# Loads, masks and the start of MLP1 rearranged in the opening of a strided sparse attention + MLP kernel

## The chip, the cores and the metric

One core of one Trainium2 chip. The metric is the device time of one execution in microseconds; the lower, the better. The engines are called PE (TensorE; PEld is its weight load), DVE (VectorE), ACT (ScalarE), POOL (GpSimd) and SP (SyncE, which only issues transfers here). [...]

## The reference

Attention over q, k and v of shape (8, 8, 576, 64): of the eight heads the first four are "local" (a row sees itself and the 31 rows before it), the last four "strided" (a row sees the rows before it at multiples of 32). Then a dense two-layer MLP over the 4608 rows.

```python
scores = scale * np.matmul(q, k.transpose(0, 1, 3, 2))
mask_local   = (rel >= 0) & (rel < 32)
mask_strided = (rel >= 0) & (pos[None, :] % 32 == pos[:, None] % 32)
scores = np.where(masks, scores, -1e9); attn = softmax(scores)
x = (attn @ v) as (4608, 512)
h = x @ w_in                      # 512 -> 2048
g = h * np.tanh(log1p(exp(h)))    # Mish
out = g @ w_out                   # 2048 -> 512
```

## The kernel before, in words

**Work.** Batch b's attention gives 576 rows of x, written transposed into a ring `xT` of four batches. The MLP goes over nine blocks t of 512 rows. `mlp1(t)` (line 435) makes h transposed in eight groups of two 512-column accumulators, eight matmuls each (two 128-row pieces of the output, four 128-deep pieces `cc` of the contraction; `cc` 2 and 3 are the strided heads, 0 and 1 the local ones), and ACT's Mish takes each group to `gT`. MLP2 of block 0 (`mlp2`, line 549) is 16 steps of four matmuls with `w_out` by its four pieces in turn (`fc_major`); blocks 1 to 8 use a seven-product scheme (`mlp2_seven`). The attention of batch t+1 is cut into steps (`attn_steps`, line 376) that are woven between the steps of block t's MLP2.

**Attention of one batch** (`class Attn`). The scores are made for short windows: strided units are 72 by 72, local ones 128 keys by 96 queries. `qk` (line 276) makes the scores of one of three parts in PSUM and ACT takes their exp into `P_s` or `P_l`; `mask` (line 298) multiplies by a 0/1 mask (DVE, or POOL in later batches); `pv` and `pv2` (lines 323, 335) make the output with the denominator as a 65th column, and DVE divides into `x_s` or `x_l`; `xt` (line 349) transposes into `xT`. q and k must first be transposed into `qTs`, `kTs`, `qTl`, `kTl`: on PE by `t_step` (line 212) and, for batch 0's local heads, `t_step_loc0` (line 244), for batches 0 and 1; by the DMA engines from batch 2 on (`transpose_by_dma`, line 185, six transfers on SP).

**Order.** Everything is issued in an order written out by hand (`manual_schedule`); each engine runs its list in that order. The opening is lines 635 to 726: SP loads batch 0's strided q and k as fp32 into `st0` (four transfers of 72 rows and two heads), its v (`vs32`, then `vl32` in two transfers), then batch 1's local q and k as fp32; POOL clears `P_l` and loads batch 0's local q and k with a cast on the way (`lq0`). DVE clears `kTs`, `P_s` and columns of ones. Then follow casts, transposes, scores, masks and outputs of batch 0, strided heads first. POOL's queue carries after that `w_in` in five pieces (held back by one-element copies into `held` until batch 0's v is cast), batch 1's strided q and k, and the first two of the four pieces of `w_out`; the rest of `w_out` and batch 2's strided q and k wait for `cast_v1` (line 728), which runs in step 0 of block 0's MLP2. On SP a small transfer `gate` (line 709) that reads the end of `w_in` holds back what stands behind it: batch 1's v, then batch 2's local q and k, then batch 2's v, and the six DMA transposes of batch 2 (put into step 9).

**PSUM.** `acc(i)` gives three accumulators of two banks, `tile_t` two tiles of one bank that transposes (`tr`, `trx`) and single outputs (`po`) share.

**MLP1 of block 0** comes after the whole attention of batch 0. Its first two groups take `cc` 2, 3 before `cc` 0, 1. Batch 1's transposes follow groups inside MLP1: local ones after the sixth and seventh, the first strided ones after the last (line 758).

Of the kernel before, what the change touches and what calls it, by code (L numbers as in the profile page):

```python
# [15 lines left out]
STRIDE = 32  # L16
# [5 lines left out]
RING = 4  # L22


def _consts():

    kk = np.arange(128)[:, None]
    qq = np.arange(WQ)[None, :]
    rel = qq + 32 - kk
    p = np.arange(PN)  # L30
    c = np.zeros((128, 128 + WQ + PN), np.float32)
    c[:, 0:128] = np.eye(128)
    c[:, 128:128 + WQ] = (rel >= 0) & (rel < STRIDE)
    c[:PN, 128 + WQ:] = (p[:, None] % 4 == p[None, :] % 4) & (p[:, None] <= p[None, :])
    return c.astype(ml_dtypes.bfloat16)
# [3 lines left out]
def kernel(ctx, tc, q, k, v, moe_w_in, moe_w_out, out):  # L39
# [15 lines left out]
    consts = const.tile([128, 128 + WQ + PN], BF16, name="consts_sb")  # L55
    ident = consts[:, 0:128]
    loc = consts[:, 128:128 + WQ]
    stm = consts[0:PN, 128 + WQ:128 + WQ + PN]
    vl32 = const.tile([128, 4, NW, D], F32, name="vl32")
# [55 lines left out]

    def load_qk_loc(b):
        for dst, src in ((kl32, k), (ql32, q)):
            if b < 2:
                nc.sync.dma_start(
                    dst[0:PL].rearrange("p h j d -> p h (j d)"),  # L120
                    src[b, 0:4].rearrange("h (p j) d -> p h (j d)", j=CL),
                )
            else:
                nc.sync.dma_start(
                    dst[0:PL].rearrange("p h i d -> p (h i) d"),
                    src[b, 0:4].rearrange("h (i p) d -> p (h i) d", p=PL),
                )
# [40 lines left out]
    def cast_qk_loc(b, e_k, e_q):  # L168
        for e, dst, src in ((e_k, kl, kl32), (e_q, ql, ql32)):
            if b < 2:  # L170
                cast(e, dst[b % 2][0:PL].rearrange("p j h d -> p h j d"), src[0:PL])
            else:
                to = by_tile(dst[b % 2])
                for hp in range(2):
                    cast(
                        e, to[:, hp].rearrange("p i e d -> p e i d"), src[0:PL, 2 * hp:2 * hp + 2]
                    )
# [34 lines left out]
    def t_step(b, kind, which, hp, eng=None):  # L212
# [17 lines left out]
        else:  # L230
            src = (ql if which == "q" else kl)[b % 2]
            for j in range(CL):
                nc.tensor.transpose(
                    tr[:, PL * j:PL * j + PL],
                    src[0:PL, j, 2 * hp:2 * hp + 2, :],
                    ident[0:PL, 0:PL],
                )
# [6 lines left out]
    def t_step_loc0(src, dst, hp, eng):  # L244

        tr = tile_t("tr")[:].bitcast(BF16)
        for j in range(CL):
            for e in range(2):
                nc.tensor.transpose(
                    tr[64 * e:64 * e + 64, PL * j:PL * j + PL], src[0:PL, 2 * hp + e, j, :],  # L250
                    ident[0:PL, 0:PL],
                )
        cast(
            eng, dst.rearrange("c (p j) -> c p j", j=CL),
            tr[:, 0:S].rearrange("c (j p) -> c p j", j=CL),
        )

    T_ORDER = [(kd, w, hp) for kd in ("s", "l") for hp in range(2) for w in ("k", "q")]

    def t_steps(b):  # L260
        return [lambda a=a: t_step(b, *a) for a in T_ORDER]
# [10 lines left out]
    class Attn:  # L272
# [3 lines left out]
        def qk(self, parts, i_acc):  # L276

            ps, o = acc(i_acc, "ps"), 0
            todo = []
            for kind, i in parts:  # L280
                w = WQ if kind == "l" else PN
                o0 = o
                for x, y in PARTS[kind][i]:
                    for e in range(2):
# [6 lines left out]
                        nc.tensor.matmul(ps[:, e, o:o + w], lhsT=lhsT, rhs=rhs, start=True, stop=True)  # L291
# [84 lines left out]
    def attn_steps(b, x, y):  # L376
# [7 lines left out]
        if x == y:  # L384
            return [
                [], [Q(x, s0)],
                [M(*s0), Q(x, s1)],
                [V("s", 0)],
                [V("s", 1), M(*s1), Q(x, *sl2)],
                [V("s", 2)],  # L390
                [V("s", 3), M("s", 2), M("l", 2), Q(x, l0)],
                [V("s", 4)],
                [V("s", 5), M(*l0), Q(x, l1)],
                [V("s", 6), V("l", 5)],
                [V("s", 7), V("l", 0), M(*l1)],
                [X("s", 0), V("l", 1)],
                [X("s", 1), V("l", 2)],
                [V("l", 3), V("l", 4)],
                [X("l", 0), X("l", 1)], [],
            ], {}  # L400
# [34 lines left out]
    def mlp1(t, accs):  # L435
# [5 lines left out]
        def group(g, ccs=(2, 3, 0, 1)):  # L441
# [20 lines left out]
            if ccs[-1] == 1:  # L462
# [3 lines left out]
                if 0 < t < B - 1 and g == 7:  # L466
# [3 lines left out]
        if t == 0:  # L470
            return gT, Sg, [lambda g=g, c=c: group(g, c) for c in ((2, 3), (0, 1)) for g in range(2)] + [
                lambda g=g: group(g) for g in range(2, 8)
            ]
# [159 lines left out]
    with tc.manual_schedule():  # L633
# [6 lines left out]
        for st, src in zip(st0, (k, q)):  # L640
            for h in (0, 2):
                nc.sync.dma_start(
                    st[:, h:h + 2, :],
                    src[0, 4 + h:6 + h].rearrange("h (p j) d -> p h (j d)", j=CS),
                )
        load_v_str(0)
        load_v_loc(0)
        load_qk_loc(1)
        lq0 = g_pool.tile([128, 16, 512], BF16, tag="Sg", name="lq0")
        lq0 = lq0[:].rearrange("p a b -> p (a b)")[0:PL]  # L650
        kl0, ql0 = [lq0[:, 1536 * i:1536 * i + 1536].rearrange("p (h x) -> p h x", h=4) for i in range(2)]
        for p in P_l:
            Po.memset(p[:], 0.0)
        for dst, src in ((kl0, k), (ql0, q)):
# [161 lines left out]
```

## Time and profile before

| | us |
|---|---|
| runs shown | 318.87, 313.11, 316.52; median 316.52 |
| the profiled execution | 314.8 |
| its span | 313.0 |
| PE busy | 291.7 |
| first PE transposes begin | 5.42 |
| PE waits for batch 0's local k until | 13.23 |
| MLP1 of block 0 begins | 25.90 |
| MLP2 of block 0 begins | 42.3 |
| MLP1 of block 1 begins | 63.5 |
| PE waits for the last DMA transpose of batch 2 until | 85.62 |

The span runs from the first to the last instruction that the profile shows; the time of the execution holds 1.8 us more. In a timeline row the first number is the start, the second the length (of a run of merged instructions: from the first start to the last end), then engine, line, operation, result<-operands and count; brackets hold the idle time of the engine before it and what ended that. A row of the waits has who waited for whom, the total, the number of times and the longest. The times of matmuls are pipelined, so that their lengths overlap; the distance of their starts tells their rate.

### The profile page before, as it was taken

What the parts mean: (1) busy time and instruction counts of PE and PEld (TensorE: products, weight loads), DVE (VectorE), ACT (ScalarE), POOL (GpSimd) and SP (SyncE); (2) the same over time, 40 slices, a digit from 0 to 9 for tenths busy, and PEclk for the clock granted to TensorE, in tenths of its full rate; (3) what the DMA queues carried; (4) which work ended last, traced back from release to release, by engine and by line L of the source; (5) the groups of instructions that cost most, each with busy time, mean ns of one, the idle gap of its engine ahead of it and who ended that gap; (6) DMA issues with size and microseconds to landing.
All of it is one profiled execution on the core that took longest, in us unless ns stands there. A gap on an engine that the chain in (4) does not pass through costs nothing.

```text
span 313.0 us, 6764 instructions
## 1 busy us (share of the span) xinstructions
PE 291.7 (93%) x2856; PEld 199.1 (64%) x2856; DVE 158.8 (51%) x362; ACT 172.8 (55%) x220; POOL 103.4 (33%) x112
## 2 busy tenths in 40 slices
PE   1678998999599999999999999999999999999995
PEld 1554454545487468746888887468745884685485
DVE  5572166866435176517642765276527652720542
ACT  3583563476454676557645765576557655514530
POOL 5486018092039402930293029202920230000000
PEclk9999999999979999999999999999999999999999
DMA  6999999999999999999999999899550011003003
GB/s 171 217 245 206 226 201 182 173 176 154 183 232 189 126 253 182 193 124 251 186 152 116 253 177 163 177 191 203 90 172 2 3 67 69 0 2 134 0 2 134
DMA packets 103261, 46.77 MB, mean 149 GB/s; under 512 B 85184, under 2 KB 96000, under 8 KB 103232
## 3 DMA queue, kind: packets, MB, share of 16 engines
q1 hardware_dynamic: 91792, 37.22, 66.1%
q0 software_dynamic: 11152, 8.92, 19.1%
q8 instruction: 22, 0.36, 0.5%
q10 hardware_dynamic: 288, 0.21, 0.2%
q14 instruction: 7, 0.06, 0.1%
HBM read 38.34 MB, written 9.44 MB: 153 GB/s over the span
## 4 chain that ended last, share of the span: by engine, by line
PE 81%; DMA 8%; DVE 4%; SPq 3%; ACT 1%; issue 1%; POOL 1%; POOLq 0%
PE psh L455 29%; PE pso L529 26%; PE psb L455 8%; PE po L318 4%; PE pso L584 4%; DMA lq<-in_k_dram 3%; PE ps L291 3%; DMA w_out<-in_moe_w_out_dram 2%; PE pso L557 2%; DMA qTl<-ql 2%; SPq L187 2%; PE trx L357 2%; SPq L193 1%; PE trx L367 1%; DVE x_l L344 1%; DVE osb L508 1%
## 5 line engine op out<-in xcount | busy, mean ns | idle before, releaser
L455 PE MATMUL psh<-xT,w_in 128*128 128x512 bf16 (+1 forms) x496 | 103.1, 361 | 0.2
L455 PEld LDWEIGHTS <-w_in 128*128 128x128 bf16 x640 | 61.8, 98 | 59.1 <-issue 2.1
L465 ACT ACTIVATE gT<-psh 128x1024 bf16<-128x1024 f32 x56 | 57.1, 1023 | 49.7 <-PE psh L455 49.7
L302 POOL TENSOR_TENSOR Pl<-Pl,consts_sb 128x960 bf16<-128x960 bf16 (+1 forms) x18 | 29.2, 1635 | 104.6 <-ACT Pl L296 104.6
L481 DVE TENSOR_TENSOR Sg<-gT 128x256 bf16<-128x256 bf16 (+2 forms) x64 | 27.0, 422 | 57.4 <-ACT gT L465 55.1
L529 PEld LDWEIGHTS <-Sg 128*128 128x128 bf16 x448 | 42.5, 99 | 6.8
L529 PE MATMUL pso<-Tw,Sg 128*128 128x256 bf16 x336 | 41.6, 279 | 0.0
L529 PEld LDWEIGHTS <-gT 128*128 128x128 bf16 x336 | 31.3, 98 | 4.7
L164 ACT COPY xT<-trx 128x576 bf16<-128x576 bf16 x32 | 20.1, 638 | 23.6 <-PE trx L367 16.7
L164 ACT COPY osb<-pso 128x512 f32<-128x512 f32 (+1 forms) x26 | 14.2, 544 | 31.7 <-PE pso L529 16.0
L455 PE MATMUL psb<-xT,w_in 128*128 128x512 bf16 (+1 forms) x144 | 30.3, 355 | 0.0
L529 PE MATMUL pso<-w_out,gT 128*128 128x256 bf16 x224 | 27.8, 272 | 0.0
L296 ACT ACTIVATE Pl<-ps 128x960 bf16<-128x960 f32 (+1 forms) x24 | 19.4, 806 | 13.9 <-PE ps L291 13.6
L508 DVE TENSOR_TENSOR osb<-pso,osb 128x512 f32<-128x512 f32 x21 | 14.5, 692 | 21.4 <-PE pso L529 21.4
L296 ACT ACTIVATE Ps<-ps 72x864 bf16<-72x864 f32 (+1 forms) x24 | 18.5, 803 | 6.0 <-PE ps L291 5.9
L461 ACT ACTIVATE gT<-psb 128x512 bf16<-128x512 f32 x32 | 19.0, 596 | 3.5 <-PE psb L455 3.5
L344 DVE TENSOR_TENSOR x_s<-po,rden 72x512 bf16<-72x512 f32 x28 | 19.2, 687 | 1.0
L302 DVE TENSOR_TENSOR Ps<-Ps,consts_sb 72x864 bf16<-72x864 bf16 (+1 forms) x24 | 13.8, 574 | 11.3 <-ACT Ps L296 10.7
L557 PE MATMUL pso<-w_out,gT 128*128 128x512 bf16 x64 | 16.4, 379 | 0.5 <-DMA w_out<-in_moe_w_out_dram 0.5
L318 PEld LDWEIGHTS <-Ps 72*128 72x128 bf16 x256 | 12.9, 103 | 5.9 <-DVE Ps L302 2.5
L318 PE MATMUL po<-vs,Ps 72*128 72x65 bf16 x256 | 14.8, 201 | 1.4 <-DVE x_s L344 0.5
L329 DVE RECIPROCAL rden<-po 96x4 f32<-96x4 f32 (+1 forms) x24 | 4.2, 177 | 22.0 <-PE po L318 21.8
(89 smaller groups left out, 341.5 us busy)
## 6 DMA issues: line engine op xcount, KB each, us to landing
out_dram<-osb SPq DMA_DIRECT2D x16, 512.0 KB, 5.1
vl<-in_v_dram SPq DMA_DIRECT2D x7, 768.0 KB
vs<-in_v_dram SPq DMA_DIRECT2D x8, 576.0 KB
kl<-in_k_dram SPq DMA_DIRECT2D x7, 576.0 KB, 9.9
ql<-in_q_dram SPq DMA_DIRECT2D x7, 576.0 KB, 13.7
w_out<-in_moe_w_out_dram POOLq DMA_DIRECT2D x4, 512.0 KB, 14.2
ks<-in_k_dram POOLq DMA_DIRECT2D x7, 288.0 KB, 5.9
qs<-in_q_dram POOLq DMA_DIRECT2D x7, 288.0 KB, 7.8
```

Source lines behind the costliest of these rows:

```text
L164: nc.scalar.copy(out_, in_)
L296: nc.scalar.activation(pt[0:n, :, 0:nw], ps[0:n, :, o0:o0 + nw], AF.Exp, scale=scale)
L302: meng.tensor_tensor(out=pm, in0=pm, in1=mk[0:n, :].unsqueeze(1).unsqueeze(1).to_broadcast([n, 2, nu, w]), op=ALU.mult,)
L318: nc.tensor.matmul(po[:, h, :], lhsT=pt[0:n, c0:c0 + 128], rhs=rhs, start=True, stop=True,)
L344: nc.vector.tensor_tensor(out=dst.rearrange("p e (h d) -> p e h d", h=4), in0=po[0:m, :, :, 0:D], in1=rden[0:m].unsqueeze(3).to_broadcast( ...
L455: nc.tensor.matmul(ps_u[:, o:o + n], lhsT=w_in[:, cc, fc * 128:(fc + 1) * 128], rhs=xT[:, cc, a:a + n], start=(cc == 2 and (o == 0 or len( ...
L461: nc.scalar.activation(gT[:, g + 8 * u, :], ps_u[:], AF.Mish)
L465: nc.scalar.activation(to, tiles[g][:], AF.Mish)
L481: nc.vector.tensor_tensor(out=out_, in0=in0, in1=in1, op=op)
L508: add = lambda o, p: nc.vector.tensor_tensor(out=o, in0=p, in1=o, op=ALU.add)
L529: nc.tensor.matmul(ps[:, pair, :], lhsT=lhs(c, 128 * pair), rhs=rhs(c), start=(first and pair == 0 and c == 0), stop=(last and c == 7), sk ...
L557: nc.tensor.matmul(p[:, ot % 2, :], lhsT=gT[:, fc, 128 * ot:128 * ot + 128], rhs=w_out[:, fc, :], start=(fc == 0), stop=(fc == 15),)
```

## The change

All of it concerns the opening, MLP1 and MLP2 of block 0 and the loads of batches 0 to 2.

- Batch 0's strided q and k are loaded, still as fp32, in pieces of 64 rows (two heads) and 8 rows (four heads); v's strided part likewise in 64 and 8 rows; `vl32` in two halves.
- Local q and k of batches 0 and 1 are loaded by POOL with the cast on the way, straight into `kl` and `ql` (`load_early_loc`); `t_step_loc0`, the fp32 loads and the casts for batch 1 are gone. `t_step`'s local branch now makes 12 transposes of 64 columns instead of 6 of 128.
- Batch 0's masks are no longer multiplied in: a matmul with the identity first puts 0 or -30000 into the PSUM tile, and the scores accumulate on it (`bias`).
- Clearing is cut to the columns that are read without being written; POOL clears no `P_l`.
- `unread(n)` adds n matmuls on a tile of zeros, whose result is not read: nine before the first transposes, two later.
- POOL's queue has one order: five pieces of w_in (released by the first half of `vl32`), first piece of w_out, batch 1's strided q, k, second piece of w_out, batch 1's local q, k, last two pieces of w_out, batch 2's strided q, k.
- SP's gate reads an earlier piece of w_in; a second gate, on w_out's third piece, holds batch 2's local q and k; batch 2's v comes after its transposes (`load_rest2`).
- MLP1 of block 0: `cc` 2, 3 of three groups (12 matmuls) are put between the local outputs of batch 0; two of batch 1's strided transposes close MLP1, the other two open MLP2, and its four local ones go into steps 5 to 8 of MLP2.

```diff
+    def by_head(x):
+        return x[0:PL].rearrange("p j h d -> p (j h d)").rearrange("p (h x) -> p h x", h=4)
+    def load_early_loc(b):
+        for dst, src in ((kl, k), (ql, q)):
+            nc.gpsimd.dma_start(by_head(dst[b]), src[b, 0:4].rearrange("h (p j) d -> p h (j d)", j=CL))
...
+    def unread(n):
+        tr = tile_t("un")
+        for _ in range(n):
+            nc.tensor.matmul(tr[:], lhsT=zeros[:, 0:128], rhs=zeros[:], start=True, stop=True)
...
+        def bias(self, kind, i, i_acc):
+            nu = len(PARTS[kind][i])
+            n, w, mb = (128, WQ, loc_bias) if kind == "l" else (PN, PN, stm_bias)
+            ps = acc(i_acc, "ps")
+            for e in range(2):
+                nc.tensor.matmul(
+                    ps[:, e, 0:nu * w].rearrange("p (u c) -> p u c", u=nu),
+                    lhsT=ident[0:n, :], rhs=mb.unsqueeze(1).to_broadcast([n, nu, w]),
+                    start=True, stop=False, skip_group_check=True,
+                )
+            return ps
...
         if x == y:
+            T = [(lambda n=n, eng=eng: t_step(b, *T_ORDER[n], eng)) for n, eng in enumerate(
+                (None, None, None, None, None, nc.scalar, None, nc.scalar))]
             return [
-                [], [Q(x, s0)],
+                T[2:4], [Q(x, s0)],
...
-                [V("s", 1), M(*s1), Q(x, *sl2)],
-                [V("s", 2)],
-                [V("s", 3), M("s", 2), M("l", 2), Q(x, l0)],
-                [V("s", 4)],
-                [V("s", 5), M(*l0), Q(x, l1)],
-                [V("s", 6), V("l", 5)],
-                [V("s", 7), V("l", 0), M(*l1)],
-                [X("s", 0), V("l", 1)],
-                [X("s", 1), V("l", 2)],
-                [V("l", 3), V("l", 4)],
-                [X("l", 0), X("l", 1)], [],
-            ], {}
+                [V("s", 1), M(*s1), Q(x, ("s", 2))],
+                [V("s", 2), T[4]],
+                [V("s", 3), M("s", 2), T[5]],
+                [V("s", 4), T[6]],
+                [V("s", 5), T[7]],
+                [V("s", 6), Q(x, l0)],
+                [V("s", 7), M(*l0), Q(x, l1)],
+                [X("s", 0), V("l", 0), M(*l1), Q(x, ("l", 2))],
+                [X("s", 1), V("l", 1), M("l", 2)],
+                [V("l", 2), V("l", 3)],
+                [V("l", 4), V("l", 5)],
+                [X("l", 0), X("l", 1)],
+            ], T[0:2]
...
         for st, src in zip(st0, (k, q)):
-            for h in (0, 2):
-                nc.sync.dma_start(st[:, h:h + 2, :], src[0, 4 + h:6 + h].rearrange("h (p j) d -> p h (j d)", j=CS))
+            src = src[0, 4:8].rearrange("h (p j) d -> p h (j d)", j=CS)
+            for p0, p1, h0, h1 in ((0, 64, 0, 2), (64, PN, 0, 4), (0, 64, 2, 4)):
+                nc.sync.dma_start(st[p0:p1, h0:h1, :], src[p0:p1, h0:h1, :])
...
+        unread(9)
+        ps = []
         for hp in range(2):
             h = 2 * hp
             cast(Dv, ks[0][0:PN, h:h + 2, :], st0[0][:, h:h + 2, :])
             t_step(0, "s", "k", hp, Sc)
+            ps.append(a.bias("s", hp, hp))
...
-        Po.tensor_copy(held[:], vs[0][0:1, 3, 0, 0:4])
+        Po.tensor_copy(held[:], vl32[0:1, 1, 5, 0:4])
         load_w_in(0, 256)
         load_w_in(256, 512)
         load_w_in(512, 1024)
-        cast_v_loc(0, Po, 0, 3)
         load_w_in(1024, 1536)
+        for h in (0, 2):
+            cast(Po, vl[0][:, :, h:h + 2, 0:D], vl32[:, h:h + 2].rearrange("p h w d -> p w h d"))
+        Po.memset(vl[0][0:32, 0, :, 0:D], 0.0)
         load_w_in(1536, 2048)
...
+        load_w_out(0, 1)
         load_qk_str(1)
-        load_w_out(0, 2)
-        nc.sync.dma_start(gate[:], w_in[0:1, 0, 1536:1792])
+        load_w_out(1, 2)
+        load_early_loc(1)
+        load_w_out(2, 4)
+        nc.sync.dma_start(gate[:], w_in[0:1, 0, 1024:1280])
         load_v(1)
...
-        a.pv2("l", 0, 1)
-        a.mask("l", 2, Dv)
-        a.pv2("l", 2, 0)
-        a.pv("l", 4)
-        a.pv("l", 5)
-        a.xt("l", 0)
+        a.pv2("l", 0, 0)
+        g1s[0]()
+        a.pv("l", 2)
+        a.pv("l", 3)
+        g1s[1]()
+        a.pv("l", 4)
+        a.xt("l", 0)
+        a.pv("l", 5)
+        g1s[2]()
         a.xt("l", 1)
...
+        load_qk_str(2)
+        nc.sync.dma_start(gate[:], w_out[0:1, 8, 0:256])
         load_qk_loc(2)
...
+        def load_rest2():
+            transpose_by_dma(2)
+            load_v(2)
+            load_qk_str(3)
+            cast_v(2, Po, Po)
```

## The prediction

> **What bounds the kernel now.** I read the page first (span, busy shares, the slices), then the table of busy time by stage, then the waits, then the timeline of the places that the waits name.
>
> ```profile
> span 313.0 us, 6764 instructions
> ...
> PE 291.7 (93%) x2856; PEld 199.1 (64%) x2856; DVE 158.8 (51%) x362; ACT 172.8 (55%) x220; POOL 103.4 (33%) x112
> ...
> PE   1678998999599999999999999999999999999995
> ```
>
> TensorE is busy 93% of the span; what it does not fill, 21.3 us, lies in the first slices, in one slice at about 80 us and at the very end. The stages (columns: length; busy us of PE, PEld, DVE, ACT, POOL; clock; DMA share; GB/s):
>
> ```profile
> 0.00:26.00 26.00, 13.75 (x221) 11.13 (x222) 15.91 (x40) 13.67 (x19) 16.71 (x26) 1.00 1.03 211
> 26.00:42.00 16.00, 16.00 (x97) 7.65 (x95) 2.85 (x4) 7.83 (x10) 2.18 (x3) 1.00 1.24 218
> 42.00:63.50 21.50, 20.31 (x236) 11.39 (x233) 15.40 (x41) 10.47 (x13) 7.79 (x11) 1.00 1.19 181
> 63.50:79.00 15.50, 15.50 (x81) 7.70 (x79) 10.37 (x17) 10.90 (x14) 9.50 (x10) 1.00 1.24 162
> 79.00:102.00 23.00, 19.48 (x247) 15.44 (x246) 10.82 (x24) 10.84 (x15) 9.92 (x9) 0.93 1.25 202
> ```
>
> The opening (attention of batch 0, until MLP1 starts) leaves PE idle 12.25 us, of which 5.4 pass before the first transposes. MLP1 (26 to 42) is full. MLP2 with batch 1's attention woven in (42 to 63.5) lacks 1.2 us. From 79 to 102 PE lacks 3.5 us. After that nothing is to be had that this change touches. The waits of PE after 42:
>
> ```profile
> PE ps L291 <- DMA qTl<-ql: 3.3, 1, 3.3
> PE pso L557 <- DMA w_out<-in_moe_w_out_dram: 0.5, 1, 0.5
> ```
>
> So the hole at 82 to 85.6 is batch 2's last DMA transpose landing late; the other is a piece of w_out. How MLP1 begins:
>
> ```profile
> 15.32 0.98 PEld L249 LDWEIGHTS <-lq 96*64 96x64 bf16 x24
> 24.90 0.99 PEld L357 LDWEIGHTS <-x_l 96*128 96x128 bf16 x12 [1.14 <-DVE x_l L330]
> 25.90 11.58 PE L455 MATMUL psh<-xT,w_in 128*128 128x512 bf16 x48
> 26.32 0.15 PEld L455 LDWEIGHTS <-w_in 128*128 128x128 bf16 x1 [0.28 <-issue]
> 26.75 0.15 PEld L455 LDWEIGHTS <-w_in 128*128 128x128 bf16 x1 [0.28 <-issue]
> 28.03 8.96 PEld L455 LDWEIGHTS <-w_in 128*128 128x128 bf16 x42 [0.28 <-issue]
> ```
>
> The weight loads stand 0.43 us apart until 28.03 and 0.213 apart after it (8.96 over 42): the first five matmuls of MLP1 run at half speed, 5 x 0.21 = 1.07 us lost. The 96-column transposes say the same: 41 ns each at 15.32, 83 ns at 24.90.
>
> **Step 1, the opening up to the end of MLP1.** Before: MLP1 ends at 41.96, by the chain of waits.
>
> Off POOL goes the clearing of P_l (2.25 us), so the two local loads are issued at about 0.75 instead of 2.94; they landed 10.3 and 11.0 us after issue, and PE waited 1.6 us for the first (until 13.23). That wait can go. What is late next is DVE: kTl's two copies (0.76 each) now stand behind the cast of vs, which began at 12.89 and took 1.23. So kTl is ready at 14.12 + 1.52 = 15.6 where ACT had it at 15.15, and q's copies end near 16.8 instead of 17.24. The masks leave DVE (0.60 x 2 + 0.45 + 0.65 x 2 + 0.35 = 3.3 us), of which the chain holds only 0.27. In their place PE gets 12 bias matmuls, 4608 columns together, at 0.216 us for 512 (MLP1's 1.73 us for 8) 1.94 us: half of them in PE's gaps of 0.6 to 0.7 us between the casts, half in front of the local scores, where ACT's copies are waited for. The nine unread matmuls (9 x 0.43 = 3.9 us) fill the empty 1.3 to 5.2, ahead of the first transposes at 5.42; without that cover they would cost what sticks out. SP issues 11 transfers, 0.42 us each, ahead of its gate instead of 9 (batch 1's two fp32 loads go, of which one held SP for 10.38); their data queue anyway. POOL casts vl behind four issues of w_in (0.75 each): 14.7 + 3.0 + 2 x 0.83 + 0.3 = 19.7, and the first local output needed it at 21.54, so 1.8 us cover it. Splitting 72 rows in 64 and 8 has no row in this trace; the four st loads released their casts 1.3 us apart, so it can be worth between +0.5 (the small pieces) and -1. I take the last product of x_s at its old time, 20.96, with -1.5 to +1.0 as bounds.
>
> From there: twelve of MLP1's 64 matmuls now run among the local outputs, 12 x 0.216 = -2.6. The half-speed start goes, -1.07. Two pairs of local transposes leave MLP1 (0.51 x 2), -1.02. The local rows are pushed: DVE has 0.89 + 4 x 0.59 instead of 2 x 0.89 + 2 x 0.59, +0.3, and of the 2.6 us of matmuls put between them PE's old gaps there (0.63 + 0.98) hide 1.6, +1.0. And the twelve may run at half speed as PE did at 24.90: between 0 and +2.6; part lies under DVE's products, I take +0.6. Sum -2.8: MLP1 ends at 39.2 (36.5 to 42).
>
> [...]
>
> **Step 2, batch 1's strided q and k.** Their first transposes now close MLP1, and in POOL's queue they stand behind w_in and a first piece of w_out. Before, w_in, ks, qs and two pieces of w_out (2048 + 576 + 1024 KB) took from the issue at 14.73 to the landing 20.6 us after 22.69, 43.3: 128 KB per us. Now 2048 + 512 + 576 KB come first: 24.5 us. The issue hangs on half of vl instead of on the cast of vs; whole vl released its cast at 17.86, the cast of vs ended at 14.12, so I leave 14.7 (13 to 18). qs is there at 39.2, when MLP1 ends (35 at the 204 GB/s that the windows from 26 to 36 show, 43 with the later issue and v of batch 1 beside it: SP's first gate opens one piece of w_in earlier, near 29 instead of 32.27). Two pieces of transposes, 0.52: MLP2 starts at 39.7 instead of 42.48, -2.8.
>
> [...]
>
> **Step 3, MLP2 of block 0.** It took 42.48 to 63.64. Four local transpose steps of 12 come in: 24 took 1.17, so +2.3. The wait for w_out (0.5) goes, as all of w_out is issued ahead: -0.5. The steps share two PSUM tiles with the outputs, and their copies (0.64 ACT, 0.76 DVE) add waits, between 0 and 4 x 0.4: I take +0.4. Sum +2.2 (+1.5 to +4).
>
> **Step 4, the hole at 82.** Batch 2's local q and k wait at a second gate (w_out's third piece, near 50) but land by the row of ql (9.9 to 13.7 us) at 61 to 65, as before (ql's cast began at 63.20). Batch 2's v now goes behind the six transposes, so their first issue no longer sits 10.03 us in a full queue, and the last, behind ql's cast of 2.7 us, can land near 72 instead of 85.6: -3.3. Then v is late next: issued near 71, landing 9 to 11 us later by the loads at 33.0 and 88.23, cast on POOL in 1.9 to 2.6, needed at 81. The new wait is 0 to 3.3; I take 0.5. Sum -2.8.
>
> **Sum:** -2.8 + 2.2 - 2.8 = -3.4. The profiled execution took 314.8 (span 313.0 and 1.8 around it): 311.4. The median of the runs shown, 316.52, stands 1.7 above that execution, the lowest, 313.11, 1.7 below.
>
> **Rivals.** (a) The hole only changes its name: v of batch 2 takes the 3.3 us. For it: SP issues v after transposes that wait for POOL; against: the queue is emptier then. -2.8 + 2.2 = -0.6: 314.2. (b) The opening is limited by its loads, and these come earlier: x_s 1.5 sooner, no half speed (0.6), no waits in MLP2 (0.4) and none at the hole (0.5): -6.4, 308.4. For it: the wait of 1.6 for the local loads; against: DVE's queue behind the cast of vs. (c) Slower: POOL's one queue falls behind PE. Behind qs come 2112 KB until w_out's last piece, which PE reaches at step 12 of 16, about 18 us later: it takes 117 KB per us. Before, w_out's second half, ks and qs (1600 KB, from 45.90 to 61.6) came at 102, w_out's piece alone (512 KB in 7.4 us) at 69, the last 1088 KB of them at 131. At 85 PE waits 6.8: 318.2. It decides below 99 KB per us, where the wait exceeds 3.4.
>
> **How the numbers follow.** Forecast 0.47 (309 to 313.5), (a) 0.20 (313.5 to 315.5), (b) 0.22 (305.5 to 309), (c) 0.11 (315.5 to 321). Leaving out the ends of (b) and (c), 306 to 317.5 holds eight in ten. Two per cent, about what a measurement of this kernel can tell from no change, is 308.5 and 321.1 against 314.8. Faster: 0.20 of (b) and 0.09 of the forecast's low end, 0.29; slower 0.04; the rest 0.67.
>
> **What would show it.** MLP1's last matmul near 39 and no half-speed spacing after it begins in earnest; no wait of PE on ks or qs over 1 us; MLP2 of block 0 some 2 us longer; no wait on a transpose of batch 2, and POOL's cast of vs done by 81. Wrong would be a long wait of PE on w_in, ks, qs, kl, ql or w_out between 22 and 62 (c), or on vs near 80 (a).

## The result, and the profile after

The changed kernel takes 336.88 us (median of 4 runs, 335.59 to 337.47), the kernel before on the same chip 317.47 (4 runs): a ratio of 1.0695, 95% interval 1.0584 to 1.0807. It is slower by 7%, where 311.4 was forecast and 317.5 was the upper end of the range. Some executions of a kernel are slower than the rest of them, so the ratios are of the others alone (of the kernel before 313.11 and 316.52) and differ from those of the medians, and of the profiled executions only e1's (322.88) is such a slow one. The profiled execution of the changed kernel took 336.94, its span 335.2, 22.2 more than the span before.

Both kernels pass the same marks on PE, so the 22.2 can be put into stages (starts of the first matmul of each MLP part in the timelines):

| stage | before | after | difference |
|---|---|---|---|
| up to the start of MLP2 of block 0 | 42.32 | 47.78 | +5.46 |
| MLP2 of block 0 | 21.16 | 41.58 | +20.42 |
| MLP1 of block 1 | 13.81 | 14.78 | +0.97 |
| MLP2 of block 1 | 22.53 | 17.42 | -5.11 |
| the rest | 213.2 | 213.6 | +0.4 |

The page shows the big loss at once, as a hole in PE's row (a slice is 8.4 us). The row PEclk is at half in two places, from 8 to 33 us and around the hole:

```profile
span 335.2 us, 6848 instructions
...
PE   5498899404899999999999999999999999999995
...
PEclk9555999955999999999999999999999999999999
```

The first of these is no loss against the kernel before. There the same row records the full clock, yet 24 transposes of local k take 1.17 us in both (at 13.23 before, at 18.31 here). Later, at full speed, twelve of this form take 0.31 of weight loads (at 55.40), and here 24 take 0.98 in both. From 11 to 28 us both kernels run at the slow rate.

PE's waits, and the timeline of PE around the longest (here and below rows of a timeline are chosen, and others may stand between two of them):

```profile
PE ps L301 <- DMA qTl<-ql: 17.6, 1, 17.6
PE tr L227 <- DVE ks L176: 5.1, 2, 4.2
PE tr L227 <- DVE qs L176: 1.8, 1, 1.8
```

```profile
62.47 0.29 PE L331 MATMUL po<-vs,Ps 72*128 72x65 bf16 x4
80.40 0.58 PE L301 MATMUL ps<-qTl,kTl 64*128 64x96 bf16 x10 [17.64 <-DMA qTl<-ql]
80.92 1.89 PE L572 MATMUL pso<-w_out,gT 128*128 128x512 bf16 x4
82.60 0.69 PE L380 MATMUL trx<-consts_sb,x_s 72*128 72x72 bf16 x8
83.09 0.42 PE L331 MATMUL po<-vl,Pl 128*128 128x65 bf16 x4
```

The instruction that waits is a local score part (L301) of batch 1, and what it waits for is a DMA transpose into qTl. The rows after it show who it belongs to: batch 1's outputs with vl follow directly. Batch 1's q and k were transposed by PE; the only DMA transposes of this stretch are batch 2's. In the listing, `load_rest2` stands in step 9 of `at`, and batch 1's second and third local score parts stand in steps 10 and 11. There is one kTl and one qTl, so in program order batch 2's transposes come first, and these two parts wait for them. They are then made from batch 2's q and k, so the changed kernel does not give batch 1's local heads the scores that the reference asks for. In the kernel before all local score parts stand in steps up to 8, ahead of the transposes.

Why the transposes are late can be read from POOL's and SP's timelines:

```profile
43.05 0.73 POOL L120 DMA_DIRECT2D qs<-in_q_dram  x1 [3.73 <-DMA ks<-in_k_dram]
61.06 1.59 POOL L176 CAST vl<-vl 128x768 bf16<-128x768 f32 x2 [17.29 <-DMA vl<-in_v_dram]
66.75 1.60 POOL L176 CAST kl<-kl 96x768 bf16<-96x768 f32 x2 [3.84 <-DMA kl<-in_k_dram]
69.11 1.60 POOL L176 CAST ql<-ql 96x768 bf16<-96x768 f32 x2 [0.77 <-DMA ql<-in_q_dram]
```

```profile
33.10 0.38 SPq L154 DMA_DIRECT2D vl<-in_v_dram  x1
55.97 0.54 SPq L752 DMA_DIRECT2D gate<-w_out  x1
56.56 0.57 SPq L130 DMA_DIRECT2D kl<-in_k_dram  x1
57.19 5.73 SPq L130 DMA_DIRECT2D ql<-in_q_dram  x1
63.08 5.00 SPq L194 DMA_TRANSPOSE kTs<-ks  x1
74.83 1.25 SPq L200 DMA_TRANSPOSE qTl<-ql  x1
```

SP's second gate waits for w_out's third piece, which POOL issued at 31.99, and held batch 2's local loads until 55.97. Batch 1's vl, issued at 33.10, landed at 61; POOL's casts of batch 2 stand behind it, but it did not decide: after it POOL still waited 3.84 us for kl and 0.77 for ql to land. The last transpose went out at 74.83 and landed 5.4 us later. From 33 to 61 POOL's queue (q0) and SP's (q1) shared the 16 engines like this (packets, MB, share):

```profile
q0 software_dynamic: 4403, 3.75, 82.2%
q1 hardware_dynamic: 4463, 1.64, 38.5%
```

SP's queue, with 256-byte rows of v, moved 59 KB per us (1.64 MB in 28 us); in the kernel before, from 33 to 48, it moved 124 (1.86 MB in 15) beside a share of 51.2% for POOL's queue. From 40 to 54 the packet counts agree, 2328 of SP's to 2333 of POOL's, and SP's queue, with the smaller packets, moved the smaller part (0.71 MB to 2.01). Before and after that the counts were not equal (366 to 1116 from 33 to 40, 1769 to 954 from 54 to 61), and the near equality of the whole is chance.

The opening's loss begins at the first casts. DVE's casts of the strided q and k, which were at 4.67, 5.95, 7.31 and 8.70:

```profile
5.35 0.69 DVE L176 CAST ks<-st 72x1024 bf16<-72x1024 f32 x1 [3.05 <-DMA st<-in_k_dram]
10.37 0.69 DVE L176 CAST ks<-st 72x1024 bf16<-72x1024 f32 x1 [4.32 <-DMA st<-in_k_dram]
13.59 0.69 DVE L176 CAST qs<-st 72x1024 bf16<-72x1024 f32 x1 [2.54 <-DMA st<-in_q_dram]
14.46 0.69 DVE L176 CAST qs<-st 72x1024 bf16<-72x1024 f32 x1 [0.18 <-DMA st<-in_q_dram]
```

Between 4 and 6 us SP's queue, on which they depend, all but stood still while the local loads of POOL ran (first fence: after; second: before, in the same 2 us):

```profile
q0 software_dynamic: 359, 0.27, 112.3%
q1 hardware_dynamic: 9, 0.02, 2.7%
```

```profile
q1 hardware_dynamic: 248, 0.43, 80.2%
q0 software_dynamic: 5, 0.00, 9.6%
```

Here the counts were far from equal, SP's 9 packets to POOL's 359. What sets the shares of the two queues is not shown.

### The profile page after: what moved, and what is told of

Same layout as the page of the kernel before. It is cut to its first block, busy times and chain, and to the rows that moved or that the text cites. A ratio compares the mean times of both kernels' runs of the same rounds, so it can differ in the third digit from the quotient of the medians.

```text
span 335.2 us, 6848 instructions
## 1 busy us (share of the span) xinstructions
PE 299.2 (89%) x2882; PEld 200.9 (60%) x2903; DVE 153.8 (46%) x363; ACT 172.3 (51%) x219; POOL 97.6 (29%) x108
## 4 chain that ended last, share of the span: by engine, by line
PE 71%; DMA 15%; issue 6%; DVE 3%; SPq 1%; POOL 1%; ACT 1%; POOLq 0%
PE pso L544 25%; PE psh L471 24%; PE psb L471 8%; DMA w_out<-in_moe_w_out_dram 7%; PE pso L599 4%; DMA ql<-in_q_dram 4%; PE po L331 3%; DMA w_in<-in_moe_w_in_dram 3%; PE ps L301 3%; DMA qTl<-ql 2%; PE trx L380 1%; SPq L200 1%; PE pso L572 1%; PE trx L370 1%; DVE x_l L357 1%
## 5 line engine op out<-in xcount | busy, mean ns | idle before, releaser
L544 PE MATMUL pso<-Tw,Sg 128*128 128x256 bf16 x336 | 40.1, 273 | 0.0
L301 PE MATMUL ps<-qTl,kTl 64*128 64x96 bf16 x192 | 9.1, 218 | 17.7 <-DMA qTl<-ql 17.6
L176 POOL CAST vl<-vl 128x768 bf16<-128x768 f32 x16 | 12.9, 836 | 17.9 <-DMA vl<-in_v_dram 17.9
L301 PEld LDWEIGHTS <-kTl 64*128 64x128 bf16 x192 | 5.4, 100 | 19.9 <-DMA kTl<-kl 17.7
```

Of the source, the lines that this page charges most:

```text
L544: nc.tensor.matmul(ps[:, pair, :], lhsT=lhs(c, 128 * pair), rhs=rhs(c), start=(first and pair == 0 and c == 0), stop=(last and c == 7), sk ...
```

## The experiments

All times below are medians beside the kernel before on the same chip (315.5 to 316.1), and the marks are of each kernel's profiled execution:

| | MLP2 of block 0 begins | it takes | MLP1 of block 1 takes | MLP2 of block 1 takes | MLP1 of block 2 begins |
|---|---|---|---|---|---|
| before | 42.32 | 21.16 | 13.81 | 22.53 | 99.82 |
| before again (b0) | 43.27 | 20.64 | 13.81 | 23.14 | 100.86 |
| after | 47.78 | 41.58 | 14.78 | 17.42 | 121.56 |
| e1 | 46.88 | 22.83 | 14.78 | 18.04 | 102.53 |
| e2 | 45.67 | 22.09 | 14.78 | 18.08 | 100.62 |
| b1 | 45.13 | 24.76 | 13.81 | 17.41 | 101.11 |
| b2 | 45.89 | 24.32 | 13.81 | 17.42 | 101.44 |
| e3 | 43.80 | 22.32 | 14.79 | 17.72 | 98.63 |
| e4 | 43.50 | 24.28 | 13.81 | 17.42 | 99.01 |
| e5 | 43.17 | 22.24 | 14.78 | 18.23 | 98.42 |
| e6 | 45.30 | 22.09 | 14.78 | 18.14 | 100.31 |
| e7 | 42.66 | 22.18 | 13.81 | 19.48 | 98.13 |
| e8 | 42.04 | 23.16 | 14.78 | 18.62 | 98.60 |
| e9 | 42.02 | 23.50 | 14.49 | 18.13 | 98.14 |

The program is nearly the same in before, b0, e4 and e7 until MLP1 ends; their 42.32 to 43.50 is what one execution differs from another in this mark. A difference of less than 1.2 us in it between two of the rows shows nothing by itself.

**e1: batch 2's transposes two steps later.**

```diff
-                at[9].append(load_rest2)
+                at[11].append(load_rest2)
```

> The changed kernel with batch 2's transposes and loads (load_rest2) moved from step 9 of block 0's MLP2 to step 11, behind the last local scores of batch 1. Order theory: PE's wait of 17.6 us came from the place of the transposes in the order alone; it goes, MLP2 of block 0 takes about 24 us instead of 41.6, and the time falls from 336.9 to about 319.5, since the opening stays 5.3 late. Rival (late loads): the loads behind are late anyway, PE waits for other pieces instead, and the time stays above 328.

Measured 319.56, ratio 1.014 (1.0083 to 1.0198). PE's wait for a DMA transpose is now 1.0 us in all and falls on a later batch, at 122.66. Batch 1's three parts come before batch 2's transposes, as in the kernel before:

```profile
60.38 0.39 PE L301 MATMUL ps<-qTl,kTl 64*128 64x96 bf16 x10
61.89 0.39 PE L301 MATMUL ps<-qTl,kTl 64*128 64x96 bf16 x10
64.31 0.26 PE L301 MATMUL ps<-qTl,kTl 64*128 64x96 bf16 x4
```

One line of order is worth 17.3 us, of 19 to 21 that the change lost. The rival, that late loads would keep it over 328, falls: loads just as late (vl at 61.4, batch 2's casts of kl and ql at 66.0 and 68.8) cost only one wait of 0.58 us, on vl, where no reader of the tiles stands behind them.

**e2: e1, and POOL clears P_l before the local loads, as before.**

```diff
+        for p in P_l:
+            Po.memset(p[:], 0.0)
         load_early_loc(0)
```

> As e1, and POOL clears P_l (2.25 us) ahead of the first two local loads, as before the change; the 64 and 8 rows stay. Contention theory: the casts of batch 0's strided q and k, at 5.35, 10.37, 13.59 and 14.46 in the changed kernel, come back to near 4.7, 6.0, 7.3 and 8.7, MLP1 ends 5 us sooner, time about 314. Rival (pieces): the small pieces of 8 rows make the loads late; the last cast stays after 13, time about 319.

Measured 317.91, ratio 1.01 (1.0055 to 1.0146); the last strided cast at 11.80 instead of 13.96 (14.46 in the changed kernel). Between the two expectations: the local loads' head start is a part of the loss, not all.

**b1: the kernel before with its local loads ahead of the clearing; b2: the kernel before with the strided q, k in 64 and 8 rows.**

```diff
+        for dst, src in ((kl0, k), (ql0, q)):
+            Po.dma_start(dst, src[0, 0:4].rearrange("h (p j) d -> p h (j d)", j=CL))
         for p in P_l:
             Po.memset(p[:], 0.0)
-        for dst, src in ((kl0, k), (ql0, q)):
-            Po.dma_start(dst, src[0, 0:4].rearrange("h (p j) d -> p h (j d)", j=CL))
```

```diff
-            for h in (0, 2):
-                nc.sync.dma_start(st[:, h:h + 2, :], ...)
+            for p0, p1, h0, h1 in ((0, 64, 0, 2), (64, PN, 0, 4), (0, 64, 2, 4)):
+                nc.sync.dma_start(st[p0:p1, h0:h1, :], src[p0:p1, h0:h1, :])
```

> The kernel before, with only the order of POOL's opening turned round: the two local loads first, the clearing of P_l after them. Contention theory: the four strided casts slip by 3 to 6 us and the time rises from 316 to about 320. Rival (pieces): the strided casts stay within 0.5 us and the wait for local k (1.6 us) goes: 314.5 to 316.

> The kernel before, with only batch 0's strided q and k loaded in 64 and 8 rows. Contention theory: the casts stay within 0.7 us, time the same within 1 us. Pieces theory: the last cast slips from 8.7 to 12 or later, time 319 or more.

Measured 315.93 (ratio 1.0051, 1.0006 to 1.0097) and 318.0 (1.0078, 1.0029 to 1.0127). The last cast moves from 8.70 to 10.53 by the first, to 11.78 by the second (b1's fence first). So each contributes; b1's 1.8 is less than its theory's 3 to 6, and its time stays in the rival's range:

```profile
10.53 0.69 DVE L166 CAST qs<-st 72x1024 bf16<-72x1024 f32 x1 [2.38 <-DMA st<-in_q_dram]
```

```profile
11.78 0.69 DVE L166 CAST qs<-st 72x1024 bf16<-72x1024 f32 x1 [2.68 <-DMA st<-in_q_dram]
```

SP's timeline suggests why the second costs: six issues take 3.8 us where four took 1.7 (b2 first, then before), so that the last of them goes out behind the start of POOL's, at 2.94. No run tries this apart from the pieces themselves.

```profile
0.75 1.99 SPq L643 DMA_DIRECT2D st<-in_k_dram  x3
2.78 1.77 SPq L643 DMA_DIRECT2D st<-in_q_dram  x3
```

```profile
0.75 0.83 SPq L642 DMA_DIRECT2D st<-in_k_dram  x2
1.62 0.83 SPq L642 DMA_DIRECT2D st<-in_q_dram  x2
```

The two add: 8.70 + 1.83 + 3.08 = 13.6, and e1 and the changed kernel, which have both, have 13.96 and 14.46. Yet neither kernel is 3 us slower in the end. MLP2 of block 0 begins 2.8 and 3.6 later in them than in the first profile and takes 3.2 to 3.6 more (with waits of 2.7 and 2.3 on w_out), but then MLP2 of block 1 takes 5.1 less: the transposes of batch 2 come at their own time, and a late PE doesn't meet them. By the start of MLP1 of block 2 only 1.3 and 1.6 us are left: a late opening of the kernel before costs little, because it ends in the hole at 82.

**e3: e1 with all that the change did to the first loads undone** (72 rows, v whole, P_l cleared on POOL first, w_in held by the cast of vs; two places of the edit are shown).

```diff
-            for p0, p1, h0, h1 in ((0, 64, 0, 2), (64, PN, 0, 4), (0, 64, 2, 4)):
+            for h in (0, 2):
...
-        Po.tensor_copy(held[:], vl32[0:1, 1, 5, 0:4])
+        Po.tensor_copy(held[:], vs[0][0:1, 3, 0, 0:4])
```

> The changed kernel with batch 2's transposes two steps later (so the stall of 17.6 us is out) and with all that the change did to the first loads undone: strided q and k in four transfers of 72 rows, v's strided part whole, its local part in one piece, P_l cleared on POOL ahead of the local loads, w_in held by the cast of vs. Bias matmuls, unread matmuls, casts in flight of batch 1, MLP1 among the outputs and the order of the weights stay. Theory (the opening lost its time by late landings alone, 64-row issues and early local packets together): the four casts stand at 4.7 to 8.8 as in the kernel before, MLP1 ends at 40 to 41, MLP2 of block 0 takes 24, no stall behind it: 312 to 314 against 316. Rival (the bias matmuls, the half clock or the one queue of POOL cost as much by themselves): casts early, but MLP1 ends past 44 all the same, 317 or more.

Measured 315.89, ratio 1.0055 (1.0007 to 1.0103): between the two. The casts stand at 4.93 to 9.38, MLP1 ends near 43.3 instead of 40 to 41. By the start of MLP2 the first loads are 3.1 to 4.0 of the opening's loss of 5.5 (e1 and after against e3), and what the change meant to gain there does not appear without that loss either.

**e4: the kernel before, with batch 2's v behind batch 2's transposes.** Step 4 alone.

```diff
-            load_v(2)
             cast_qk_loc(2, Po, Po)
-            load_qk_str(3)
-            cast_v(2, Po, Po)
+        def load_rest2():
+            transpose_by_dma(2)
+            load_v(2)
+            load_qk_str(3)
+            cast_v(2, Po, Po)
...
-                at[9].append(lambda: transpose_by_dma(2))
+                at[9].append(load_rest2)
```

> The kernel before with one thing of the change: batch 2's v (and what followed it on POOL) is issued after batch 2's transposes. Step 4 of the prediction by itself. By it the hole of 3.3 us at 82 goes and up to 0.5 of a wait on v comes: 312.9 to 313.6 against 316 (ratio near 0.991). Rival (a): v of batch 2 is late in its place, and PE waits for vs at 80 to 86 as long: 315.5 to 316.5.

Measured 313.88, ratio 0.9976 (0.9936 to 1.0017): not told from no change. The hole at 82 is gone and no wait on v came, so rival (a) falls. What the order did is seen at the last transpose: issued at 72.18 instead of 79.16, it landed near 74.8 instead of 85.6. The missing hole alone would not show it, since PE came to these scores at 86.41 instead of 82.11; b1 and b2, with the old order, lose the hole in that way. The hole in the kernel before, with what follows it:

```profile
85.62 0.22 PE L291 MATMUL ps<-qTl,kTl 64*128 64x96 bf16 x2 [3.30 <-DMA qTl<-ql]
85.77 3.36 PE L529 MATMUL pso<-Tw,Sg 128*128 128x256 bf16 x16
```

The sixteen matmuls behind the wait take 3.36 us, at half speed, against 1.92 elsewhere. In e4 the gain went to a wait some 25 us earlier:

```profile
56.22 1.02 PE L557 MATMUL pso<-w_out,gT 128*128 128x512 bf16 x4 [2.20 <-DMA w_out<-in_moe_w_out_dram]
58.00 1.49 PE L557 MATMUL pso<-w_out,gT 128*128 128x512 bf16 x3 [0.32 <-issue]
59.74 1.69 PE L557 MATMUL pso<-w_out,gT 128*128 128x512 bf16 x4
```

From 58.0 to 61.5, behind the wait of 2.20, four matmuls take up to 1.7 us instead of 1.02. MLP2 of block 0 is 3.1 longer than before: 1.7 of it is the longer wait, the other 1.4 is about what the half speed costs.

**e5: e3 without the eleven unread matmuls.**

```diff
-        unread(9)
...
-                unread(2)
```

> e3 without the eleven unread matmuls. Theory by the trace of the changed kernel (granted clock 0.50 from 10 to 30 us in spite of them): they change nothing after the casts, within 0.5 us of e3. Rival (they hold the full clock where the casts are early): the first transposes, scores and outputs run at half speed without them, 1 to 2.5 us more than e3.

Measured 315.64, ratio 1.0017 (0.9975 to 1.0059), not told from e3 by the median. The recorded clock differs: from 10 to 30 us it is at half with them and at full without. It is the third number from the end of each row (first e3, then e5):

```profile
10.00:20.00 10.00, 7.53 (x118) 5.06 (x118) 4.78 (x9) 4.01 (x6) 4.69 (x7) 0.50 1.21 197
```

```profile
10.00:20.00 10.00, 7.16 (x119) 5.07 (x118) 5.20 (x9) 3.84 (x7) 4.28 (x7) 1.00 1.16 190
```

But the matmuls from 10 to 20 us run alike, as the middle rows show; the outer rows show where the two differ (again first e3, then e5):

```profile
7.11 0.43 PE L227 MATMUL tr<-consts_sb,ks 72*128 72x72 bf16 x8 [0.50 <-DVE ks L176]
14.34 1.17 PE L241 MATMUL tr<-consts_sb,kl 96*64 96x96 bf16 x24 [1.98 <-DMA kl<-in_k_dram]
27.07 1.90 PE L471 MATMUL psh<-xT,w_in 128*128 128x512 bf16 x4
```

```profile
7.32 0.66 PE L227 MATMUL tr<-consts_sb,ks 72*128 72x72 bf16 x8
14.76 1.17 PE L241 MATMUL tr<-consts_sb,kl 96*64 96x96 bf16 x24 [1.97 <-DMA kl<-in_k_dram]
27.40 1.02 PE L471 MATMUL psh<-xT,w_in 128*128 128x512 bf16 x4
```

With the unread matmuls eight transposes at 7.11 run at full speed (0.43), without them at half (0.66). By 10.13 that was gone in e3 too (eight in 0.66), and from there to 27 both run at half speed, whatever the record says. Then full speed comes later in e3: four matmuls of MLP1 take 1.90 at 27.07, in e5 1.02 at 27.40. MLP2 of block 0 begins at 43.80 with the unread matmuls and at 43.17 without. In these two executions the unread matmuls thus gain a little before 10 us and lose more after 27; in the medians neither is seen. Of e3's ten executions seven record a mean clock of 0.962 to 0.967 and three 0.995 or more; their times, 314.2 to 317.4 and 315.1 to 318.0, do not follow the record.

**e6: e3 with the twelve matmuls of MLP1 behind the outputs.**

```diff
-        g1s[0]()
...
+        g1 = g1s + g1
```

> e3 with the twelve matmuls of MLP1 behind the local outputs again instead of among them. By the prediction's terms (-2.6, +1.0 of pushed rows, +0.6 of half speed) it takes 1.0 us more than e3; by the other bound of these terms (half speed for all twelve) nothing, or 0.5 less. Rival (batch 1's strided q and k or w_out land too late for MLP1's earlier end to count): no difference within 0.3, and a wait of PE on ks or w_out over 1 us in e3.

Measured 315.74, ratio 1.0064 (1.0018 to 1.011), the same as e3. By the marks the twelve among the outputs gain 1.50 at the start of MLP2 (45.30 to 43.80), a little more than the scatter of this mark, and 1.68 at MLP1 of block 2. In the profiled execution of e3 this went again in MLP2 of block 2: PE waited 1.87 there and then ran at half speed (sixteen matmuls in 3.56 instead of 1.92), because a copy on ACT waited 3.28 for an output's store, issued on SP behind batch 3's transposes. That the other executions of e3 lose it in the same place is not shown.

**b0, the kernel before again, and e7: e4 with all of w_out issued at once.**

```diff
-        load_w_out(0, 2)
+        load_w_out(0, 4)
...
             Po.tensor_copy(held[:], vs[1][0:1, 3, 0, 0:4])
-            load_w_out(2, 4)
             load_qk_str(2)
```

> The kernel before, unchanged, a second profile. The undisturbed marks of the first profile: MLP2 of block 0 from 42.32, 21.16 long with a wait of 0.5 on w_out; MLP2 of block 1 takes 22.53, 5.1 more than the 17.42 of other kernels (3.3 of wait, 1.6 to 1.8 at half speed behind it); MLP1 of block 2 at 99.82. One theory: these marks repeat within 0.3, and the 2.2 to 2.7 of wait on w_out in the variants of it comes of their edits. Rival: the two waits exchange places from one execution to the next (more on w_out, less at 82), MLP1 of block 2 between 99 and 101 either way.

> e4 (the kernel before, batch 2's v issued after batch 2's transposes) with the last two pieces of w_out issued right behind the first two instead of after the cast of batch 1's v. Theory (the gain of the hole was given back to the wait on w_out and the half speed behind it): no wait of PE on w_out, MLP2 of block 0 in 21.2 to 21.8 instead of 24.3, MLP1 of block 2 at 95.5 to 96.5; time 310.5 to 312.5 against 315.5. Rival (w_out in front starves batch 1's v, as it was from 33 to 61 in the changed kernel): PE waits for vl by 2 to 5 us instead, 314 to 316.

b0, a single execution, took 315.87 and repeats the hole (3.1, MLP2 of block 1 in 23.14), with no wait on w_out; its other marks differ from the first profile's by up to 1.0, not 0.3. In two executions, then, the hole and the wait on w_out did not exchange places. e7 measured 315.16, ratio 0.9982 (0.9948 to 1.0015): the rival holds. The wait on w_out is gone, and one on vl is there, as long:

```profile
PE po L318 <- POOL vl L166: 2.3, 1, 2.3
```

```profile
57.33 0.29 PE L318 MATMUL po<-vl,Pl 128*128 128x65 bf16 x4 [2.25 <-POOL vl L166]
57.46 1.02 PE L557 MATMUL pso<-w_out,gT 128*128 128x512 bf16 x4
```

Behind this wait PE runs at full speed at once (1.02 for four), unlike in e4, so MLP2 of block 0 takes 22.18. In this stretch the transfers set the pace; the orders tried only chose who waits. The five profiled executions with w_out in its old place show it: in before and b0 PE waits 0.5 or less for w_out, and POOL casts batch 2's ql at 63.2 and 63.8; in e4, b1 and b2 it waits 2.2 to 2.7 for w_out, and ql is cast at 55.5 to 57.6. Why the one or the other lands first, in e4 against b0 with w_out issued at nearly the same time (47.09 and 46.85), was not settled.

**e8: e5 with the masks multiplied and the constants at 74 KB instead of 116; e9: e8 with a transpose of x_l one step earlier.**

```diff
-            ps.append(a.bias("s", hp, hp))
...
-            a.qk([("s", i)], None, ps[i])
+            a.qk([("s", i)], i)
+        a.mask("s", 0, Dv)
...
-    c = np.zeros((128, 128 + 2 * (WQ + PN)), np.float32)
+    c = np.zeros((128, 128 + WQ + PN), np.float32)
```

```diff
-                [V("l", 4), V("l", 5)],
-                [X("l", 0), X("l", 1)],
+                [X("l", 0), V("l", 4), V("l", 5)],
+                [X("l", 1)],
```

> e5 with the masks of batch 0 multiplied in on DVE again and the constants without the two bias tables (74 KB instead of 118). By the prediction's step 1 bias matmuls cost 1.0 beside what they hide under and the masks 0.27 on the chain: MLP2 of block 0 begins 0.5 to 0.8 earlier than in e5 (42.4 to 42.7 against 43.17). If the larger constants are what holds the first casts back (5.13 in e5, 4.67 in the kernel before), the first cast stands at 4.7 and the last at 8.8 instead of 9.8, and 0.5 to 1 more is gained. Rival (the masks on DVE are in the chain of the local outputs): MLP2 of block 0 begins at 44 or later, 1 us more than e5.

> e8 with the first of the two last transposes of batch 1's local rows one step earlier (ahead of the last two local outputs). In the changed kernel and all variants of it MLP1 of block 1 takes 14.78 instead of 13.81, with a wait of 0.81 on ACT's copy of these rows after its first four matmuls. Theory (the change's new order of the last steps put both transposes right ahead of MLP1, so that two copies of 0.64 lie in the open): one copy remains, the wait falls to 0.1 to 0.4, MLP1 of block 1 to 13.9 to 14.4, the time by 0.4 to 0.8 to 312.6 to 313.0. Rival (the last local outputs' division is late anyway, so the remaining transpose waits for it as long): no difference within 0.2.

e8 measured 313.42, ratio 0.9955 (0.9924 to 0.9986); e9 313.52, ratio 0.9945 (0.9912 to 0.9978). These are the versions that are faster than the kernel before, by half a per cent. In e8 the last cast stands at 8.87 instead of 9.80. In the three runs with the two tables of the bias and otherwise old first loads (e3, e5, e6) it stands at 9.38 to 9.80, in e8 without them at 8.87, each time released by a load of st; in e9, also without them, it stands by an estimate near 8.5, since the transposes behind it begin at 9.25 where e8's begin at 9.61. So the tables (42 KB more, on ACT's queue, in the same first 4 us: in the changed kernel issued at 0.8 and landed 2.1 later; the expectation's 118 KB is 116) go with strided loads that land 0.5 to 1.3 later:

```profile
8.87 0.69 DVE L172 CAST qs<-st 72x1024 bf16<-72x1024 f32 x1 [0.72 <-DMA st<-in_q_dram]
```

MLP2 begins 1.13 earlier, within what both terms together lead to expect (1.0 to 1.8) and within the scatter of this mark; how it divides between the tables and the matmuls was not measured. By MLP1 of block 1 only 0.2 of it is left, and MLP1 of block 2 begins no earlier (98.60 against 98.42), so these marks do not show where e8's lower time comes from. e9's wait fell by 0.29, MLP1 of block 1 to 14.49, and MLP2 of block 0 grew by 0.34, since the transpose now waits among the outputs: no gain, the rival's side.

## Why the prediction was wrong

- **Step 3 and step 4, the placing of the transposes: the step that failed, 17.64 of 22.2.** Step 3 priced the waits that the new order of MLP2 brings at 0 to 1.6, taken +0.4, and saw them in two PSUM tiles and their copies. The tiles that mattered were kTl and qTl: one wait for them took 17.64. Step 4 read `load_rest2` only for what is late at 82: "Batch 2's v now goes behind the six transposes". It did not set the transposes against batch 1's local scores, which the same diff moved from steps 4, 6 and 8 to 9, 10 and 11. This can be seen without a time, by laying the new steps beside the position of `load_rest2`. e1 shows it: 17.3 us by one line.
- **Step 4, the hole: right, and mis-sized.** By e4 the new order brings the last transpose from 85.6 to about 74.8, where "near 72" was forecast, and no wait on v came. In the changed kernel it landed at 80.2, since the second gate opened at 55.97, not near 50, and kl and ql were there at 66.7 and 69.1, not 61 to 65; its missing hole is no proof, since PE came to it 27 us late. The hole was worth -5.11, not -2.8: besides 3.3 of wait it had 1.8 behind it, most of it the half speed at 85.77. But e4 by itself brings only 0.8 of span, and no change that is clear of noise, as w_out takes its place.
- **Step 1, x_s "at its old time, 20.96", bounds -1.5 to +1.0: failed.** The last product of x_s is at 27.9, +7.0. The step set the price of 64 and 8 rows as "between +0.5 and -1"; it is +3.1 on the last cast (b2). It counted the early local loads as a wait removed, but not what their packets do to the loads beside them: +1.8 (b1). It left out that the constants grow by 42 KB: 0.5 to 1.3 (e3, e5, e6 against e8, e9).
- **Step 1 behind x_s: the right sign, half the size.** From x_s's end to the end of MLP1 -2.8 was forecast; 21.0 became 19.5, -1.5. The "half speed for the twelve" was larger than the 0.6 taken: eight of the twelve ran at half speed, about 1.7. The interleaving by itself gains 1.5 (e6), where -2.6, +1.0 and +0.6 make -1.0.
- **The clock.** The prediction took the row of 24.90 for half speed, rightly (twelve weight loads in 0.99, where six take 0.28 to 0.38 later), and that of 15.32 for full speed. This was wrong: those transposes are of another form, 64 columns instead of 128, and ran at half speed too, 24 weight loads in 0.98 where twelve take 0.31 at 55.40 in the changed kernel. The kernel before runs at half speed from its first transposes (0.66 for eight, 0.42 at 41.80) to 28.03, so its rows show no full clock that was lost. e3 shows one: with the nine unread matmuls full speed came early (eight transposes in 0.43 at 7.11, against 0.66 in e5), and it was gone by 10.13 with no idle of PE over 0.7 us between. Waits of 1.87 (e3) and 2.20 us (e4) were followed by half speed too, and ones of 1.79 (e2) and 2.25 (e7) were not; what decides which was not tried.
- **Step 2: its rate was right, and that PE did not wait was luck.** PE did not wait for ks or qs, and MLP2 began 0.35 behind MLP1. From the issue of w_in to the landing of qs it took 25.0 us, where 24.5 was forecast (24.3 to 24.7 in e3 and e8). But the issue came at 19.03, not at 14.7 (13 to 18), since vl's first half landed late, and qs was there at 44.0, not 39.2; a PE at its forecast time would have waited nearly 5 us. The lower bound of 35 does not come out of its numbers either: 3136 KB at 204 GB/s from 14.7 give 30.4. **Rival (c) did not come** as it was told, for PE never waited for w_out. But its cause, a POOL queue that crowds, did: w_out's third piece, issued at 31.99, held the second gate until 55.97, and with it the transposes.
- **Step 3 without the wait:** +0.9 to +1.7 (e1, e2, e3: 22.83, 22.09 and 22.32 against 21.16), +2.8 in the changed kernel with half speed behind the stall; +2.2 was forecast. Its price of the four local steps, 2.3, was taken from rows at half speed; at full speed a step of 12 takes 0.38 (59.81 to 60.19), four 1.5. Not seen at all: the two transposes of x_l now directly ahead of MLP1 of block 1, +0.97.

The size of the failed step is explained; that the opening gains nothing even with its old first loads (MLP2 of block 0 at 42.0 to 43.8 in e3, e5, e8 and e9, where 39.7 was forecast) is explained only in part, by the half speed, the tables and the scatter named above.

## What to carry to other kernels

When a change moves both the writer of a tile and its readers, write the new program order of every tile with a single buffer first, and only then cost the waits: here the transposes, placed ahead of two readers' last use, made these wait 17.64 us for them, and read the wrong data. A load is not free for being early: in this opening, which waits for its first transfers, more issues on the same queue and an earlier load on another delayed the one that is waited for (by 3.1 in b2, 1.8 in b1), and larger constants most likely did (0.5 to 1.3 in e3, e5 and e6 against e8 and e9). And where transfers set the pace, a hole that is closed can open at the next of them, as in e4 (2.20 on w_out) and e7 (2.25 on vl): compare the mark behind the stage, not the wait.

## What the runs showed of the hardware

- A transfer of 64 or of 8 rows held SP longer per issue than one of 72 rows: 0.49 to 0.76 us each in b2, 0.33 to 0.44 in before. What sets that was not tried.
- SP's queue stood nearly still for 2 us while POOL's first local loads ran (9 packets beside 359, in the changed kernel from 4 to 6), though from 40 to 54 us the two queues moved nearly the same number of packets (2328 beside 2333).
- Behind 3.3 (before), 2.20 (e4) and 1.87 us (e3) of PE's waiting, matmuls ran at half speed for 3 to 4 us (sixteen in 3.36 and 3.56 instead of 1.92 in before and e3, four in up to 1.7 instead of 1.02 in e4). Behind 2.25 (e7) and 1.79 (e2) they ran at full speed (four in 1.02, sixteen in 1.92).
- With the unread matmuls (e3) PE ran at full speed to some 9 us (0.43 for eight transposes), then at half until 29; without them (e5) at half speed from the first (0.66 for eight) to about 27.
- The recorded clock was no measure of the rate in the opening: e5 records 1.00 from 10 to 20 us and e3 0.50, and the same 24 transposes take 1.17 in both.
